# A list schedule made with other DMA constants and a pause between two engines' port operations

## The chip, the cores and the metric

The kernel runs on one core of a Trainium2 chip. The metric is the device time of one execution in microseconds (us), and a kernel's time is the median of its runs. Matrix products run on TensorE (PE in the rows), elementwise work and reductions on VectorE (DVE), ScalarE (ACT) and GpSimd (POOL); SyncE (SP) issues the DMA transfers in the order of its queue.

## The reference

One transformer-like block over 2048 tokens of 512 features: a layer norm, linear attention with a learned feature map (32 heads of 16), and a gate from a two-layer network of width 1792.

```python
def _A_ref(x, wqkv, w_phi, wo):
    qkv = (lambda x, *d: x.transpose(*d))((x @ wqkv).reshape(B, S, 3, H, Dh), 2, 0, 3, 1, 4)
    q, k, v = qkv[0], qkv[1], qkv[2]
    pq = jnp.einsum("bhsd,hdf->bhsf", q, w_phi)
    pk = jnp.einsum("bhsd,hdf->bhsf", k, w_phi)
    phi_q = jnp.concatenate([_softmax(pq, axis=-1), _softmax(-pq, axis=-1)], axis=-1)
    phi_k = jnp.concatenate([_softmax(pk, axis=-1), _softmax(-pk, axis=-1)], axis=-1)
    kv = jnp.einsum("bhsf,bhsd->bhfd", phi_k, v)
    z  = jnp.einsum("bhsf->bhf", phi_k)
    num = jnp.einsum("bhqf,bhfd->bhqd", phi_q, kv)
    den = jnp.einsum("bhqf,bhf->bhq", phi_q, z)[..., None] + 1e-6
    o = num / den
    return (lambda x, *d: x.transpose(*d))(o, 0, 2, 1, 3).reshape(B, S, D) @ wo
def _B_ref(x, w1, b1, w2):
    h = jnp.einsum("bsd,df->bsf", x, w1) + b1
    sp = jnp.log1p(jnp.exp(-jnp.abs(h))) + jnp.where(h > 0, h, jnp.zeros_like(h))
    return jnp.einsum("bsf,fd->bsd", h * jnp.tanh(sp), w2)
xn = _layernorm(x, axis=-1)
s = _A_ref(xn, A_wqkv, A_w_phi, A_wo)
g = _silu(_B_ref(xn, B_w1, B_b1, B_w2))
return x + s * g
```

## The kernel before

The kernel doesn't issue its instructions as it meets them. A class `Program` records every operation with its tiles, the engines that could do it, and what each would cost; `links` finds what depends on what; `simulate` plays the program through a model of the engines and gives every operation a start; `issue` then emits them in the order of these starts. All of them are emitted from one line, L372 (L371 in the changed kernel), so the rows are told apart by tiles.

The order has two levels. The string `ORDER` names the parts of the work, and TensorE does them in just that order. For the other engines, and for operations that either VectorE or GpSimd could do, the model decides, by when an operation is wanted. An operation that GpSimd is given gets a wait on the last VectorE operation that uses the port that the two share, when its planned start lies within `NEAR` ns of that one's end.

The parts that matter here: `N` normalizes a block of 128 tokens and transposes it on TensorE (tiles `x`, `st`, `mv`, `rs`, `nb`, `pt`); `Ka` to `Kd` are the k and v projections of a pair of blocks, built of seven products in place of eight from sums of weights (`ws1` to `ws4`, the v halves `wv0` and `wv1`) and differences of tokens (`xs`); `wk` and `wq` fold the feature map into the weights on TensorE (`wkf`, `wqf`). `A` accumulates k times v (`kvp`), `Q` projects q (`qx`, `qy`, `qz`), `D` and `U` are denominator and numerator (`pn`), `O` the output projection (weights `wor`, split in `wo`). `P` prepares a block of the first network weights (`w1a`, split in `w1ah`, `w1al`, `w1sh`, `w1sl`) and stores it, `M` loads it again (`w1b`), `Fa` to `Fd` are the four steps of the first network layer (`fx`, `fy`, `fz`; results `ha`, `hb`, `hc`, `hd`), `G` the second, `E` the end. Every product of two fp32 tiles is three matmuls of a high half and a low half: `fh` and `fl` are the halves of the transposed tokens, and `L` loads those of the second 1024 tokens from where they were stored (`xd`).

Tiles come out of pools with a fixed number of places. TensorE's accumulators are eight banks, used in turn: a product must wait until the engine that reads the bank's former content is done. Loads go into a pool of 38 places, and a load waits in SyncE's queue for the last reader of what its place held; what stands behind it in that queue waits too.

Of the kernel before, what the change touches and what calls it, by code (L numbers as in the profile page):

```python
# [27 lines left out]
NC = 8  # L28
PEN, HOLD, MARGIN, PTOL = -1000, 300, 1000, 0
BACK, COLD, DRATE, LANES, SWITCH = 1500, 3400, 300, 8, 300  # L30
BLOCK, HEAD, FETCH, IDLE = 256, 89, 5200, 2100
# [3 lines left out]
SLACK, AHEAD, LAT = 15000, 40000, 150  # L35
WAKE, NEAR = 13, 2500
ORDER = """
wk0 N6 N0 wv1 N1 wk1 wv0 N2 Ka0 Ka1 N3 ws Kb0 N7 b1 Kc0 N4 Kd0 wq0 wq1 N5 Kb1 P0 Kc1 Fa0 Kd1 A0 Ka2 Kb2 Kc2 Fb0 N8 N9
N10 Kd2 A1 Ka3 Kb3 Fc0 Kc3 N11 Kd3 N12 P5 A2 Ka4 Fd0 Kb4 Fa5 Fb5 Kc4 A3 N14 P4 Ka5 Fc5 Kd4 Kb5 Kc5 Fd5 N13 Fa4 Kd5 Fb4
A4 Fc4 N15 Ka6 Kb6 A5 Ka7 Kc6 Kb7 P3 P2 P6 Kc7 Kd7 Fa6 Kd6 Fa3 Fa2 Fb3 wQ Fb6 M0 Fc3 Fc6 Fd4 A6 P1 A7 Fa1 Fb2 Fd3 Q0  # L40
Fd6 Fc2 z D0 Fb1 Fc1 D1 L Q3 Q1 D2 Q2 Fa7 D3 Fb7 Fd1 Fd2 D4 M1 Q4 M3 Fc7 Fa10 Fd7 Fa8 D5 Fb8 D6 Fc8 M2 Fd8 D7 Fb10 Q7
M6 Fa9 D8 M5 Fc10 M4 Fb9 Q5 Fd10 Fc9 Q6 D9 Fa13 Fd9 Fa12 D10 Ub0 Fb13 Fb12 D11 Fc13 Fc12 D12 wo0 Fa11 wo1 Fb11 D13 Ua0
D14 Fc11 Fd13 O1 O4 O6 O7 R1 O0 O3 O5 R2 R0 Fd11 Fd12 G7 D15 Ua1 R4 G8 O2 Ub1 G14 G15 R5 O9 O15 O10 O8 G9 G16 R3 G17
G10 G11 R6 G12 G18 G19 G13 E1 G0 O14 G1 G20 E2 G2 O13 G3 G4 O11 G28 G5 G29 G30 G6 G31 G32 G33 G34 G35 E0 G21 G36 G22
G23 G24 E4 G37 G38 G39 G40 G41 G25 G42 G26 O12 E5 G27 G43 G44 G45 G49 E3 G46 G50 G47 G48 G51 E6 E7
"""
# [7 lines left out]
class Program:  # L54
# [105 lines left out]
    def links(self):  # L160
        ops = self.ops
        wr, rd = {}, {}
        for o in ops:
            o.succ, dep = [], set()
            for n in o.reads:
# [7 lines left out]
            if "PE" in o.impl:  # L173
                dep = {d for d in dep if "PE" not in ops[d].impl}
# [17 lines left out]
    def simulate(self, at):  # L192
# [20 lines left out]
        aset = 0  # L213
        half = False
        dma = port = told = 0
        code, fetched, cold = HEAD, 0, 0
# [24 lines left out]
        def go(o, e):  # L241
            nonlocal aset, dma, port, half, code, fetched, cold
            dur, calls = o.impl[e]
# [21 lines left out]
            if e in o.lock:  # L265
                dur += max(0, port - now)
                port = now + dur
            o.start, o.eng = now, e
# [5 lines left out]
            if e == "Q":  # L274
                if not lanes:
                    dur = 0
                    busy[e] = now
                nb = calls[0][1][0].free_size() * calls[0][1][0].shape[0] * 4
                dma = max(dma, now + (1100 if now > 2500 else 1350)) + nb / DRATE
                end = max(dma + 1000, now + 2000 + nb / 200)  # L280
                lanes.append(end)
                heapq.heappush(events, (dma - BACK, 2, -1))
# [16 lines left out]
        while left:  # L299
# [34 lines left out]
            for e in ("A", "V", "G", "Q"):  # L334
# [3 lines left out]
                while ready[e]:  # L338
                    late, i = heapq.heappop(ready[e])
                    o = ops[i]  # L340
                    if o.start is not None:
                        continue
                    if e in o.lock and port > now + PTOL:
                        held = True
                        skip.append((late, i))
                        if len(skip) > 60:
                            break
                        continue
# [31 lines left out]
def locks(e, m, a):  # L380
# [732 lines left out]
```

## Time and profile before

| what | value |
|---|---|
| time, median of 3 runs | 501.36 us (500.89 to 501.74) |
| time of the profiled execution | 501.55 us |
| its span, from the first to the last instruction | 499.8 us |
| TensorE busy | 487.7 us |
| VectorE, ScalarE, GpSimd busy | 443.6, 282.4, 271.1 us |
| moved by DMA | 105.69 MB, mean 211 GB/s |
| mean granted clock of TensorE | 0.991 |

The span is some 1.7 us shorter than the execution's time. Busy times of matmuls include a modelled end, so that those of successive matmuls overlap; how far apart they start is what one costs. The granted clock is a share of full speed (2.4 GHz); 0.50 is the lower level, 1.2 GHz.

### The profile page before, as it was taken

What the parts mean: (1) busy time and instruction counts of PE and PEld (TensorE: products, weight loads), DVE (VectorE), ACT (ScalarE), POOL (GpSimd) and SP (SyncE); (2) the same over time, 40 slices, a digit from 0 to 9 for tenths busy, and PEclk for the clock granted to TensorE, in tenths of its full rate; (3) what the DMA queues carried; (4) which work ended last, traced back from release to release, by engine and by line L of the source; (5) the groups of instructions that cost most, each with busy time, mean ns of one, the idle gap of its engine ahead of it and who ended that gap; (6) DMA issues with size and microseconds to landing.
All of it is one profiled execution on the core that took longest, in us unless ns stands there. A gap on an engine that the chain in (4) does not pass through costs nothing.

```text
span 499.8 us, 10023 instructions
## 1 busy us (share of the span) xinstructions
PE 487.7 (98%) x3690; PEld 424.3 (85%) x3690; DVE 443.6 (89%) x830; ACT 282.4 (57%) x433; POOL 271.1 (54%) x204
## 2 busy tenths in 40 slices
PE   8699999999999999999999999999999999999996
PEld 8478888878888889888898878778998899999996
DVE  6989999989999999999999989989587899768875
ACT  4676666445365552535243664487356888758611
POOL 4669997689688154889559497643020312112200
PEclk9799999999999999999999999999999999999999
DMA  8524438646979879888766286462644846644742
GB/s 303 185 92 161 148 97 297 220 190 171 358 287 321 298 257 337 306 274 285 251 216 231 100 289 225 170 211 94 201 133 148 269 150 191 207 150 139 255 154 85
DMA packets 68641, 105.69 MB, mean 211 GB/s; under 512 B 6896, under 2 KB 37744, under 8 KB 68592
## 3 DMA queue, kind: packets, MB, share of 16 engines
q1 hardware_dynamic: 68448, 104.79, 62.1%
q8 instruction: 29, 0.48, 0.4%
q10 hardware_dynamic: 144, 0.26, 0.2%
q14 instruction: 20, 0.16, 0.1%
HBM read 60.60 MB, written 44.43 MB: 210 GB/s over the span
## 4 chain that ended last, share of the span: by engine, by line
PE 91%; DVE 6%; ACT 2%; issue 1%; DMA 0%; DVEq 0%; ACTq 0%
PE y L372 28%; PE fx L372 15%; PE pw L372 9%; PE kx L372 8%; PE fy L372 7%; PE qx L372 5%; PE ky L372 4%; PE fz L372 4%; PE qy L372 2%; PE pn L372 2%; PE kz L372 2%; PE kvp L372 1%; PE pt L372 1%; PE qz L372 1%; PE wake L372 1%; PE wqf L372 1%
## 5 line engine op out<-in xcount | busy, mean ns | idle before, releaser
L372 POOL TENSOR_TENSOR r<-r 128x128 f32<-128x128 f32 (+1 forms) x18 | 10.2, 576 | 95.3 <-DVE r L372 56.6
L372 ACT ACTIVATE ah<-r 128x896 fp32r<-128x896 f32 (+1 forms) x56 | 46.8, 854 | 18.0 <-DVE r L372 9.4
L372 DVE TENSOR_TENSOR al<-r,ah 128x896 fp32r<-128x896 f32 (+1 forms) x45 | 46.3, 1047 | 9.1 <-ACT ah L372 4.9
L372 DVE TENSOR_TENSOR r<-r 128x128 f32<-128x128 f32 (+1 forms) x102 | 36.2, 384 | 6.8 <-ACT r L372 5.1
L372 ACT ACTIVATE r<-r 128x512 f32<-128x512 f32 x56 | 34.1, 624 | 14.1 <-DMA r<-hd 12.4
L372 PE MATMUL y<-w2t,ah 128*128 128x256 f32 x224 | 41.0, 283 | 0.0
L372 PE MATMUL fx<-fh,w1b 128*128 128x512 f32 x112 | 38.5, 392 | 0.0
L372 PEld LDWEIGHTS y<-w2t,ah 128*128 128x128 f32 x224 | 34.9, 192 | 0.2
L372 PE MATMUL y<-w2t,al 128*128 128x256 f32 x112 | 31.7, 283 | 0.0
L372 POOL TENSOR_TENSOR al<-r,ah 128x896 fp32r<-128x896 f32 (+1 forms) x11 | 20.1, 1829 | 21.0 <-ACT ah L372 9.5
L372 PE MATMUL y<-w2h,ah 128*128 128x256 f32 x96 | 27.2, 283 | 0.0
L372 PE MATMUL y<-w2l,ah 128*128 128x256 f32 x96 | 27.2, 283 | 0.0
L372 PE MATMUL y<-w2h,al 128*128 128x256 f32 x96 | 27.1, 283 | 0.0
L372 PEld LDWEIGHTS fx<-fh,w1b 128*128 128x128 f32 x112 | 21.0, 188 | 5.0 <-DVE ha L372 0.4
L372 PE MATMUL fx<-fl,w1b 128*128 128x512 f32 x56 | 21.9, 390 | 0.0
L372 PEld LDWEIGHTS y<-w2t,al 128*128 128x128 f32 x112 | 21.5, 192 | 0.2
L372 ACT ACT_TABLE_LOAD x13 | 16.7, 1283 | 6.9 <-DVE yy L372 5.5
L372 PE MATMUL y<-w2g,al 128*128 128x256 f32 x72 | 20.4, 283 | 0.0
L372 PE MATMUL y<-w2m,ah 128*128 128x256 f32 x72 | 20.4, 283 | 0.0
L372 PE MATMUL y<-w2g,ah 128*128 128x256 f32 x72 | 20.4, 283 | 0.0
L372 PE MATMUL fy<-fh,w1b 128*128 128x512 f32 x56 | 19.5, 389 | 0.0
L372 ACT ACTIVATE hb<-fx,b1t 128x512 f32<-128x512 f32 x14 | 9.6, 689 | 17.0 <-PE fx L372 14.5
(735 smaller groups left out, 1837.8 us busy)
## 6 DMA issues: line engine op xcount, KB each, us to landing
r<-hd SPq DMA_DIRECT2D x56, 256.0 KB, 3.5
xd<-xc SPq DMA_DIRECT2D x8, 896.0 KB, 5.5
w1b<-w1d SPq DMA_DIRECT2D x14, 512.0 KB, 4.6
w1b<-w1d SPq DMA_DIRECT2D x14, 384.0 KB, 4.3
so<-so SPq DMA_DIRECT2D x16, 256.0 KB, 2.6
x<-x SPq DMA_DIRECT2D x15, 256.0 KB, 4.0
w1a<-w SPq DMA_DIRECT2D x7, 512.0 KB, 5.4
w1d<-w1sh SPq DMA_DIRECT2D x7, 512.0 KB, 2.8
```

The lines of the kernel that those rows point to most:

```text
L372: ins = getattr(e, m)(*a, **k)
```

## The change

The string `ORDER` is another one, and the model that orders the other engines has other numbers. A transfer is planned to take its bytes at 400 instead of 300 bytes per ns and to land 1150 ns after that, where it was the later of 1000 ns after it and 2000 ns plus the bytes at 200 per ns after the issue; rows with short runs count as more bytes. `PTOL` is gone: after a VectorE operation that uses the shared port, GpSimd is now planned to start one only 140 ns (`GUARD`) after its end, and VectorE's are no longer stretched in the plan. `NEAR` goes from 2500 to 4000. `links` makes every operation on a tile of the pools depend on the tile's first operation. The instructions themselves stay as they were: TensorE has 2669 rows in both orders, SyncE 312 transfers in both, VectorE 815 and then 814.

```diff
-PEN, HOLD, MARGIN, PTOL = -1000, 300, 1000, 0
-BACK, COLD, DRATE, LANES, SWITCH = 1500, 3400, 300, 8, 300
+PEN, HOLD, MARGIN, GUARD = -1000, 300, 1000, 140
+BACK, COLD, DRATE, LANES, SWITCH = 1500, 3400, 400, 8, 300
-WAKE, NEAR = 13, 2500
+WAKE, NEAR = 13, 4000
 ORDER = """
-wk0 N6 N0 wv1 N1 wk1 wv0 N2 Ka0 Ka1 N3 ws Kb0 N7 b1 Kc0 N4 Kd0 wq0 wq1 N5 Kb1 P0 Kc1 Fa0 Kd1 A0 Ka2 Kb2 Kc2 Fb0 N8 N9
...
+wk0 N0 b1 N2 N1 N6 wv1 wk1 wv0 Ka1 ws Ka0 wq1 N3 Kb0 N7 N10 Kc0 P0 Kd0 N4 Kb1 N5 Kc1 Kd1 Fa0 Fb0 Fc0 A0 Ka2 Kb2 Kc2
...
     def links(self):
-        wr, rd = {}, {}
+        wr, rd, head = {}, {}, {}
         for o in ops:
-            o.succ, dep = [], set()
+            o.succ, dep = [], {head.setdefault(n, o.idx) for n in o.tiles if self.tag.get(n, "ps") != "ps"}
...
             if e in o.lock:
-                dur += max(0, port - now)
-                port = now + dur
+                port["V"], port["G"] = now + dur, now + dur + (GUARD if e == "V" else 0)
...
-                nb = calls[0][1][0].free_size() * calls[0][1][0].shape[0] * 4
-                dma = max(dma, now + (1100 if now > 2500 else 1350)) + nb / DRATE
-                end = max(dma + 1000, now + 2000 + nb / 200)
+                dma = max(dma, now + (1100 if now > 2500 else 1350)) + volume(calls[0][1]) / DRATE
+                end = dma + 1150
...
-                    if e in o.lock and port > now + PTOL:
+                    if e in o.lock and port[e] > now:
...
+def volume(aps):
+    runs = []
+    for v in aps[:2]:
+        n = 1
+        for st, c in reversed(list(v.ap)):
+            if st != n:
+                break
+            n *= c
+        runs.append(n)
+    return aps[0].free_size() * aps[0].shape[0] * (4 if min(runs) > 128 else 4.7)
```

The first place is TensorE's start, behind the first two foldings of the k weights. Before, three blocks of tokens are transposed (`pt`), then the other two foldings (`wkf`), then a fourth block:

```order
4 L372 MATMUL pt_151<-ident,x_146 128x128 x4
5 L372 MATMUL pt_157<-ident,x_152 128x128 x4
6 L372 MATMUL pt_166<-ident,x_161 128x128 x4
7 L372 MATMUL wkf_172<-phit,wkT_141 128x128 x4
8 L372 MATMUL wkf_173<-phit,wkT_142 128x128 x4
9 L372 MATMUL pt_182<-ident,x_177 128x128 x4
10 L372 MATMUL kx_183<-wv0h,fl_106 128x512
11 L372 MATMUL kx_183<-wv0l,fh_105 128x512
```

In the changed order all four blocks come ahead of the foldings:

```order
4 L371 MATMUL pt_151<-ident,x_146 128x128 x4
5 L371 MATMUL pt_157<-ident,x_152 128x128 x4
6 L371 MATMUL pt_163<-ident,x_158 128x128 x4
7 L371 MATMUL pt_171<-ident,x_166 128x128 x4
8 L371 MATMUL wkf_178<-phit,wkT_141 128x128 x4
9 L371 MATMUL wkf_179<-phit,wkT_142 128x128 x4
10 L371 MATMUL kx_183<-wv0h,fl_106 128x512
11 L371 MATMUL kx_183<-wv0l,fh_105 128x512
```

The foldings `wkf` stand closer to the first `kx`, and with them the copies that empty their banks.

The second place is VectorE at the first of these copies, the low half `wkl` of a folded k weight. Before, it stands as number 44, behind row statistics:

```order
40 L372 BN_STATS st_209<-x_208 128x6
41 L372 BN_AGGR mv_210<-st_209 128x2
42 L372 TENSOR_SCALAR rs_211<-mv_210 128x1
43 L372 BN_STATS st_221<-x_220 128x6
44 L372 TENSOR_TENSOR wkl_170<-wkf_172,wkh_169 128x512
45 L372 TENSOR_SCALAR nb_191<-mv_189,rs_190 128x1
46 L372 BN_AGGR mv_222<-st_221 128x2
47 L372 TENSOR_SCALAR rs_223<-mv_222 128x1
48 L372 BN_STATS st_240<-x_239 128x6
49 L372 TENSOR_TENSOR wkl_170<-wkf_173,wkh_169 128x512
```

In the changed order it is number 41:

```order
33 L371 BN_AGGR mv_204<-st_203 128x2
34 L371 TENSOR_SCALAR rs_205<-mv_204 128x1
35 L371 BN_STATS st_213<-x_212 128x6
36 L371 BN_STATS st_221<-x_220 128x6
37 L371 BN_AGGR mv_214<-st_213 128x2
38 L371 BN_AGGR mv_222<-st_221 128x2
39 L371 TENSOR_SCALAR rs_215<-mv_214 128x1
40 L371 TENSOR_SCALAR rs_223<-mv_222 128x1
41 L371 TENSOR_TENSOR wkl_176<-wkf_178,wkh_175 128x512
```

It has moved ahead by three places; of the two splits of v weights, the one of `wv0` has come to VectorE and the one of `wv1` has gone to GpSimd.

The third place is SyncE's queue where the token halves of the second 1024 tokens are loaded (`fh`, `fl` from `xd`). Before:

```order
100 L372 DMA hd_480<-hd_550 128x512
101 L372 DMA hd_551<-hc_535 128x512
102 L372 DMA fh_572<-xd 128x1024
103 L372 DMA kvw<-kvd 32x4x256
104 L372 DMA fl_573<-xd 128x1024
```

In the changed order the first low half `fl_612` stands there, and its place in the pool held `w1al_440`:

```order
101 L371 DMA hd_503<-hd_568 128x512
102 L371 DMA kvw<-kvd 32x4x256
103 L371 DMA fh_611<-xd 128x1024
104 L371 DMA hd_580<-ha_579 128x512
105 L371 DMA fl_612<-xd 128x1024
106 L371 DMA fh_613<-xd 128x1024
107 L371 DMA fl_614<-xd 128x1024
108 L371 DMA w1b_639<-w1d_443 128x768
```

On TensorE the last product with `w1al_440` is followed by two more of its kind and a q projection:

```order
739 L371 MATMUL fx_507<-fh_117,w1al_440 128x512
740 L371 MATMUL fx_507<-fl_118,w1ah_439 128x512
741 L371 MATMUL fx_507<-fh_117,w1ah_439 128x512
742 L371 MATMUL qx_598<-wqh_525,fl_106 128x256
743 L371 MATMUL qx_598<-wql_526,fh_105 128x256
```

Then comes the first reader of `fl_612`:

```order
781 L371 MATMUL qx_598<-wq1h,fl_118 128x256
782 L371 MATMUL qx_598<-wq1l,fh_117 128x256
783 L371 MATMUL qx_598<-wq1h,fh_117 128x256
784 L371 MATMUL fx_628<-fh_611,w1b_517 128x512
785 L371 MATMUL fx_628<-fl_612,w1b_516 128x512
786 L371 MATMUL fx_628<-fh_611,w1b_516 128x512
```

In the string, three q projections stand between `L` and `Fa7` before, and none in the changed one; there three matmuls of 128x512 and the last q projection lie between the release of the place and the reader.

## Rows read from the trace of the kernel before

**Rows 1.** The page, busy us, share of the span and instructions of two engines.

```profile
PE 487.7 (98%) x3690; PEld 424.3 (85%) x3690; DVE 443.6 (89%) x830; ACT 282.4 (57%) x433; POOL 271.1 (54%) x204
```

**Rows 2.** What TensorE waited for: us in all, times, longest.

```profile
PE kx L372 <- DVE wkl L372: 3.1, 1, 3.1
PE pt L372 <- ACT x L372: 2.2, 3, 1.1
PE wake L372 <- DVE mhalf L478: 1.1, 1, 1.1
PE kx L372 <- POOL wv0l L372: 1.0, 1, 1.0
```

**Rows 3.** Two windows: length, busy us by engine, granted clock, DMA share, GB/s.

```profile
20.00:26.00 6.00, 4.82 (x11) 3.84 (x12) 5.88 (x12) 1.98 (x4) 4.09 (x4) 0.50 0.02 4
...
120.00:480.00 360.00, 360.00 (x2732) 316.20 (x2731) 322.56 (x578) 206.89 (x310) 176.46 (x121) 1.00 0.68 227
```

**Rows 4.** TensorE's timeline: start, us, what; in brackets the idle time before it.

```profile
17.68 0.40 PE L372 MATMUL kz<-wv1h,fh 128*128 128x512 f32 x1
21.18 0.77 PE L372 MATMUL kx<-wv0h,fl 128*128 128x512 f32 x1 [3.10 <-DVE wkl L372]
...
30.99 0.66 PE L372 MATMUL pt<-ident,x 128*128 128x128 f32 x4 [1.06 <-ACT x L372]
31.41 0.48 PE L372 MATMUL kx<-ws3h,fl 128*128 128x512 f32 x1
...
41.49 0.39 PE L372 MATMUL ky<-ws1h,fl 128*128 128x512 f32 x1
```

**Rows 5.** VectorE's timeline, 16 to 24 us.

```profile
16.49 1.22 DVE L372 TENSOR_TENSOR ws<-ws,wvr 128x1024 f32<-128x1024 f32 x1
17.63 0.42 DVE L372 TENSOR_TENSOR fl<-xs,fh 128x256 fp32r<-128x256 f32 x1
17.96 0.42 DVE L372 TENSOR_TENSOR fl<-pt,fh 128x256 fp32r<-128x256 f32 x1
...
19.76 0.68 DVE L372 BATCH_NORM_STATS2 st<-x 128x6 f32<-128x512 f32 x1
20.36 0.67 DVE L372 TENSOR_TENSOR wkl<-wkf,wkh 128x512 fp32r<-128x512 f32 x1
...
23.56 1.61 DVE L372 TENSOR_TENSOR ws<-wvr,ws 128x1024 f32<-128x1024 f32 x1
```

**Rows 6.** The chain that ended last, in order of time: start, us, what.

```profile
36.26 3.57 PE wqf L372 x32
...
271.88 2.69 PE pn L372 x115
```

**Rows 7.** TensorE's timeline around the first q projection.

```profile
172.39 0.28 PE L372 MATMUL qx<-wqh,fl 128*128 128x256 f32 x1
...
177.55 0.40 PE L372 MATMUL fx<-fh,w1al 128*128 128x512 f32 x1
177.79 0.40 PE L372 MATMUL fx<-fl,w1ah 128*128 128x512 f32 x1
```

**Rows 8.** DMA issues of the whole trace: times, KB each, median us to landing.

```profile
w1b<-w1d SPq DMA_DIRECT2D x14, 512.0 KB, 4.6
...
fl<-xd SPq DMA_DIRECT2D x7, 512.0 KB, 6.6
...
wor<-wo SPq DMA_DIRECT2D x2, 512.0 KB, 4.8
```

**Rows 9.** The same view of the load issued at 199.67 us alone.

```profile
fl<-xd SPq DMA_DIRECT2D x1, 512.0 KB, 3.8
```

**Rows 10.** The same view of the load issued at 192.09 us alone.

```profile
fl<-xd SPq DMA_DIRECT2D x1, 512.0 KB, 8.1
```

**Rows 11.** The same view of the second load of the output weights, 286.83 us.

```profile
wor<-wo SPq DMA_DIRECT2D x1, 512.0 KB, 5.7
```

More of the change, by code (lines that the diff above doesn't have):

```diff
@@ L35 @@
 SLACK, AHEAD, LAT = 15000, 40000, 150
-WAKE, NEAR = 13, 2500
+WAKE, NEAR = 13, 4000
 ORDER = """
-wk0 N6 N0 wv1 N1 wk1 wv0 N2 Ka0 Ka1 N3 ws Kb0 N7 b1 Kc0 N4 Kd0 wq0 wq1 N5 Kb1 P0 Kc1 Fa0 Kd1 A0 Ka2 Kb2 Kc2 Fb0 N8 N9
[L39 to L45, printed above, removed]
+wk0 N0 b1 N2 N1 N6 wv1 wk1 wv0 Ka1 ws Ka0 wq1 N3 Kb0 N7 N10 Kc0 P0 Kd0 N4 Kb1 N5 Kc1 Kd1 Fa0 Fb0 Fc0 A0 Ka2 Kb2 Kc2
+Fd0 P5 Kd2 A1 Ka3 N11 N8 Fa5 Kb3 N9 P4 N12 Kc3 Fb5 Fc5 A2 Fd5 Kd3 Ka4 Fa4 Kb4 Kc4 Kd4 N13 Fb4 A3 Ka5 Kb5 Kc5 Kd5 Fc4
+Fd4 P6 Fa6 A4 N14 N15 P1 Ka6 Kb6 wq0 P3 A5 Ka7 Kc6 Kd6 Kb7 P2 Kc7 Kd7 Fb6 Fa3 Fb3 Fa1 A6 Fb1 Fc6 Fc1 M0 Fc3 A7 wQ Fd6
+Q0 Q1 z Fd3 D0 D1 Fa2 Q2 Fd1 D2 Q3 L D3 Fa7 D4 Fb2 Fc2 M1 Fa8 Fd2 Fb7 M3 D5 Fb8 Fc8 D6 M6 Fc7 Q4 Fd7 D8 Fa10 Fd8 Fb10
+M2 Q7 Q5 Q6 Fa13 Fa9 Fb13 Fb9 D7 Fc10 Fc13 D9 D10 wo1 D11 M4 Fc9 Ua0 Fd13 Fd9 Fa11 Fb11 wo0 M5 R0 Fd10 Fa12 D12 Fb12
+Fc11 Fc12 Ub0 Fd12 R1 Fd11 D13 G7 O3 O5 O0 O7 R2 O2 O1 D14 R3 O6 D15 Ub1 O4 G8 Ua1 R6 R5 G0 G1 G9 O13 R4 O14 G10 G2
+G11 G3 G4 G12 G5 G6 G13 G14 E0 O9 O12 G15 G16 G17 G18 G19 G28 G20 G29 E1 E2 O15 O10 O8 G30 G42 G31 G32 G33 G43 G34 O11
+G35 G44 E4 G36 G21 G45 G46 G22 G47 G48 G37 G23 G38 E6 G39 G40 G24 G25 G26 G41 G27 E5 E3 G49 G50 G51 E7
 """
@@ L214, in simulate @@
         half = False
-        dma = port = told = 0
+        dma = told = 0
+        port = {"V": 0, "G": 0}
         code, fetched, cold = HEAD, 0, 0
@@ L241, in go @@
         def go(o, e):
-            nonlocal aset, dma, port, half, code, fetched, cold
+            nonlocal aset, dma, half, code, fetched, cold
             dur, calls = o.impl[e]
@@ L359, in simulate @@
                     heapq.heappush(ready[e], s)
-                if held and port > told:
-                    told = port
-                    heapq.heappush(events, (port, 2, -1))
+                if held and port[e] > told:
+                    told = port[e]
+                    heapq.heappush(events, (told, 2, -1))
         return sorted(ops, key=lambda o: (o.start, o.idx))
```

## The prediction

> **What bounds the kernel now.** I read the page's busy shares first: TensorE is busy for 487.7 of 499.8 us, VectorE for 443.6 [rows 1]. So a change of order can only give back what TensorE does not work, and the next view, what TensorE waited for, says how little that is: four entries, 7.4 us in all, the longest 3.1 us for VectorE's copy `wkl` and three waits of together 2.2 us for normalized rows `x` [rows 2]. The windows say where: from 20 to 26 us the granted clock is 0.50, the lower of its two levels, and from 120 to 480 us TensorE is busy for all of 360.00 us [rows 3]. Its timeline of the start shows the mechanism. The last product of `kz` starts at 17.68; the next `kx`, at 21.18, needs an accumulation bank in which a folded weight `wkf` still lies, and VectorE empties it only with `wkl`. What is at stake is thus the start (some 7 us of waits and the slow stretch behind the longest of them), against the risk of opening a wait in a stretch that has none.
>
> **The change, part by part.** No instruction is added or taken away that counts. The constants act through the order alone, so I follow the order at two places.
>
> *The start, VectorE.* In before, VectorE reaches `wkl` at 20.36 and ends it at 21.03, and TensorE starts 0.15 us later [rows 4, 5]. In the changed order `wkl` comes after fewer things. Steps cost 1.14 us (128x1024), 0.60 (128x512 and a row statistic) and 0.33 (128x256), which are the distances between starts [rows 5]; the smallest ones I put at 0.1. From the first sum `ws`, which I place at 9.9, nineteen instructions stand ahead of `wkl`: two, five and six of the three sizes and six small ones, 2.3 + 3.0 + 2.0 + 0.6 = 7.9 us, 17.8. With 0.7 us for waits on rows that land I take 18.5, and 19.25 for TensorE's second `kx`: 1.9 us earlier than 21.18. By itself this is a lead of 1.9 us.
>
> *The start, what is late next.* The changed order has two things more before TensorE's product with `ws3h`: two of the four folds of the q weights (four take 3.57 us in before [rows 6], so 1.79) and one more transposition (0.42 from 30.99 to 31.41 [rows 4]). I carry the chain on with the same prices: TensorE comes to `ws3h` at about 31.1. Before, it is there at 31.41, having done 2.2 us less: a lead of 2.5 us. But then its transposition of row block 4 takes the bank that VectorE empties with the fortieth instruction after `wkl`, a subtraction into `xs`. Ahead of that stand three of 1.14, thirteen of 0.60, fourteen of 0.33, one of 0.44 (a scaling of 512 columns, my estimate from its neighbours) and nine small ones: 3.4 + 7.8 + 4.6 + 0.4 + 1.0 = 17.2. From 18.5 that is 35.7, and 36.0 at its own end; with 0.4 for short waits on ScalarE and GpSimd I take 36.4. TensorE would have been ready at 35.3, so 1.1 us are lost there. Four more instructions (2.2 us) lead to the addition into `v1`, which releases the bank for `ky` with `ws1h`, at 38.65. Before, that product starts at 41.49, after all four folds [rows 4]; with 1.79 us for the two not yet done, the lead is 41.49 − 38.65 − 1.79 = **1.05 us**. Its bounds: 2.5 if VectorE is not late (the copies then being a little faster than I counted), 0 if it loses another microsecond. I take 1.0, since all steps are rows of the same form. The folds that were put off stand later on TensorE and cost there what they save here.
>
> *The middle, the reload of the tokens.* In before the first low half of the second token half, `fl_573`, is asked for some 21 us of matmuls (counted along the order) ahead of its first reader. In the changed order `fl_612` stands in SyncE's queue behind the last product with `w1al_440`, whose place it takes, and its first reader comes soon: two more products of 128x512, one q projection of 42 products, one product. A product is 0.24 us (177.55 to 177.79) and a q projection with its change of form 5.16 us (172.39 to 177.55) [rows 7], so 0.48 + 5.16 + 0.24 = 5.9 us. The load takes 6.6 us in the median of seven [rows 8]; 3.8 at the front of a burst [rows 9] and 8.1 inside one [rows 10]. With 0.1 us to issue, TensorE waits 0.8 us by the median, nothing by the fast end, 2.3 by the slow one. `fl_612` stands near the front of its burst (only `fh_611` goes well ahead of it), so I take **0.5**.
>
> *The middle, the output weights.* The second load of `wo` now stands one group of `pn` (2.69 us [rows 6]) and eighteen products (4.32) ahead of the product that waits for what ScalarE does behind it: a 128x1024 split and one eviction, some 1.7 us (my estimate from VectorE's 1.14 and 0.60 for such sizes). 7.0 − 0.1 − 1.7 leaves 5.2 for a load that takes 4.8 in the median of its two [rows 8] and 5.7 as the slower of them [rows 11]. Bounds are 0 and 0.5; I take **0.2**.
>
> *The planned pause.* VectorE operations that ran into GpSimd's are visible: a `ws` of 128x1024 took 1.61 us against a distance of 1.14 for its like [rows 5]. TensorE waits for VectorE nowhere after the start [rows 2], so time that VectorE gains there is worth nothing at the end, and 0.14 us of pause cost nothing either, as GpSimd has the slack. Covered by the same fact: instructions moved between the two engines. If that cover is gone, a collision of half a microsecond shows in full.
>
> *Sum.* The profiled execution took 501.55 us: 499.8 of span and 1.75 around it. −1.0 (start) + 0.5 (tokens) + 0.2 (`wo`) gives 501.25, and as that execution lies 0.19 above the median of 501.36, **501.1** for a median.
>
> **The rule of the Trainium skill that bears on this.** The page "DMA: Bandwidth & Descriptors", section "Anatomy of one DMA — SWDGE (gpsimd) path", gives 2.0 us and bytes/436e3 for one transfer, an estimate of 3.2 us for the 512 KB of `fl`. It is stated for another queue than the one here. By it both waits of the middle would be nothing and the sum 500.4. The trace disagrees: no load of that size has a median under 4.6 us, and `fl` has 6.6 [rows 8].
>
> **The rivals.** *Faster:* the reloads land as at the front of the burst (3.8 us [rows 9]); the start keeps its 1.0 and the time is 500.4; if VectorE is also in time at row block 4, the lead is 2.5 and the time 498.9. For it speaks that the changed burst begins with the queue nearly empty; against it that further loads follow within a few microseconds. Chance 0.31.
>
> *Slower, by one mechanism:* the schedule now believes that a lone load of 512 KB lands 3.6 us after it is issued (1100 + 524288/400 + 1150 ns), while before it believed 4.6 (2000 + 524288/200), and the rows say 4.6 to 6.6 [rows 8]. So loads stand late in the queue, and TensorE waits for the first reader of `fl_612`. At 8.1 us [rows 10] that wait is 2.3, and with 0.5 at `wo` the time is 501.36 − 1.0 + 2.3 + 0.5 = 503.2. It decides from a landing of some 7.6 us on: there the wait is 1.8, and with 0.2 at `wo` it outweighs the lead of 1.0 by the 1.0 that can be told. Against it: most such loads land sooner. A place that I did not follow, where VectorE's work is now needed earlier, would look the same in the total. Chance 0.27.
>
> *No change:* the lead of the start is returned in the middle, in whole or for the greater part, or never arises; 500.4 to 502.4. This is my forecast's own case, chance 0.42.
>
> **How the numbers follow.** A measurement of this kernel can tell about 0.2%, 1.0 us, from no change. The forecast 501.1 lies within that of 501.36, its own range 500.4 to 502.3. Faster than 500.36 is the first rival, slower than 502.36 the second: 0.31, 0.42, 0.27. The range leaves out a tenth at each end: 499.2 (a little short of the whole lead of the start) and 503.2 (both loads at their slow ends).
>
> **What the profile after would show.** Right: `wkl` on VectorE near 18.5 and the second `kx` near 19.3; a wait of about 1 us of a transposition for VectorE near 35 us; `ky` with `ws1h` near 38.7; waits of TensorE for `fl<-xd` near 198 us and for ScalarE near 275 us, together about 0.7 us. Wrong: TensorE waiting in the first 10 us for the second part of the k weights, whose load now goes out one row block later; no wait at row block 4; a wait for the reload above 2 us; or a wait for VectorE in the stretch from 120 to 480 us, where the order before has none.

## The result, and the profile of the changed kernel

The changed kernel takes **503.11 us** in the median of 7 runs (502.11 to 503.67), the kernel before 500.89 beside it (499.62 to 501.74, 7 runs): a ratio of 1.0047, interval 1.003 to 1.0065, so slower by some 2 us. A second measurement (e1 below) gives 1.0046 (1.0027 to 1.0065). The forecast was no change, 501.1, which is 0.3 below the 501.36 that it started from; the kernel went up by 2.2, as its slower rival says. That 503.11 still lies inside the range (499.2 to 503.2), at its upper end, is owed to the base: 501.36 is 0.5 to 1.8 us above the medians of the kernel before in all later measurements.

Executions of the kernel before come in two kinds by clock: of the fourteen beside e1, nine have a mean granted clock of 0.994 to 0.999 and take 499.5 to 501.0 us, and five, like the one that the prediction was read from (501.55, 0.991), have 0.991 or 0.992 and take 501.2 to 502.0.

The profiled execution of the changed kernel took 502.11 us (span 500.3), the least of its seven. The page's busy line, against [rows 1]: TensorE does the same work, VectorE 4.6 us less, and nothing came of it.

```profile
PE 487.8 (98%) x3690; PEld 423.5 (85%) x3690; DVE 439.0 (88%) x833; ACT 278.2 (56%) x430; POOL 269.7 (54%) x204
```

What TensorE waited for, against [rows 2]. The wait for `wkl` is only 0.5 us shorter; two waits for `xs` are new, and one for ScalarE's eviction `hd`.

```profile
PE kx L371 <- DVE wkl L371: 2.6, 1, 2.6
PE wqf L371 <- DVE xs L371: 1.6, 1, 1.6
PE wake L371 <- DVE mhalf L490: 1.1, 1, 1.1
PE pt L371 <- ACT x L371: 0.8, 2, 0.6
PE pt L371 <- DVE xs L371: 0.8, 1, 0.8
PE fz L371 <- ACT hd L371: 0.5, 1, 0.5
```

The windows, against [rows 3]: 20 to 26 us at a mean of 0.72, and half a microsecond lost where there had been none.

```profile
20.00:26.00 6.00, 4.89 (x19) 3.73 (x17) 5.91 (x15) 2.75 (x5) 3.46 (x3) 0.72 0.00 0
120.00:480.00 360.00, 359.51 (x2795) 315.20 (x2795) 317.51 (x577) 205.58 (x313) 172.26 (x120) 1.00 0.65 222
```

TensorE's timeline at the places of [rows 4], taken from the trace of e5 (the changed kernel but for three instructions near 278 us, which do not bear on the start), where the clock of this stretch was full:

```profile
16.34 0.39 PE L383 MATMUL kz<-wv1h,fh 128*128 128x512 f32 x1
19.37 0.47 PE L383 MATMUL kx<-wv0h,fl 128*128 128x512 f32 x1 [2.64 <-DVE wkl L383]
...
26.50 1.13 PE L383 MATMUL wqf<-phit,wqT 128*128 128x128 f32 x8 [2.28 <-DVE xs L383]
...
31.44 0.48 PE L383 MATMUL kx<-ws3h,fl 128*128 128x512 f32 x1
...
36.67 0.63 PE L383 MATMUL pt<-ident,x 128*128 128x128 f32 x4 [0.90 <-DVE xs L383]
...
38.83 0.50 PE L383 MATMUL ky<-ws1h,fl 128*128 128x512 f32 x1 [0.15 <-DVE v L383]
```

In the changed kernel's own trace, with the clock at 0.72, VectorE comes to `wkl` as forecast:

```profile
18.55 0.68 DVE L371 TENSOR_TENSOR wkl<-wkf,wkh 128x512 fp32r<-128x512 f32 x1
```

The second `kx` starts at 19.37 too, `ws3h` at 31.46, the transposition at 36.66 and `ky` at 38.81. The start is therefore as it was worked out (19.25, 31.1, 36.4, 38.65), and it does not depend on TensorE's clock: what TensorE gains at full clock it gives back as a longer wait for `xs` (2.28 instead of 1.6). VectorE sets it.

DMA issues of the whole trace, against [rows 8]: `w1b` has gone from 4.6 to 6.2.

```profile
w1b<-w1d SPq DMA_DIRECT2D x14, 512.0 KB, 6.2
w1b<-w1d SPq DMA_DIRECT2D x14, 384.0 KB, 6.3
fl<-xd SPq DMA_DIRECT2D x7, 512.0 KB, 6.1
wor<-wo SPq DMA_DIRECT2D x2, 512.0 KB, 5.4
```

Two windows show what goes with it; the last three columns are granted clock, DMA share and GB/s. First the changed kernel:

```profile
200.00:240.00 40.00, 40.00 (x211) 34.51 (x210) 38.51 (x74) 15.31 (x24) 35.32 (x24) 1.00 1.01 383
260.00:290.00 30.00, 29.53 (x246) 23.45 (x245) 28.80 (x54) 14.05 (x24) 19.63 (x12) 1.00 0.83 270
```

Then the kernel before:

```profile
200.00:240.00 40.00, 40.00 (x225) 35.11 (x224) 37.82 (x70) 19.57 (x30) 34.56 (x25) 1.00 0.86 293
260.00:290.00 30.00, 30.00 (x267) 24.94 (x266) 28.25 (x56) 14.50 (x26) 21.97 (x15) 1.00 0.55 194
```

The changed order packs the traffic of the middle into 200 to 240 us and fills the DMA engines there entirely (in the windows of 20 us beside it the share is 0.47 ahead and 0.12 behind, against 0.91 and 0.65 before). The loads of `w1b` of 512 KB that lie in this window land after 6.7 us in the median, and after 5.3 in the kernel before.

The reload that the forecast priced is not late: `fl_612` lands 3.9 us after its issue, 1.8 us ahead of its first reader, which follows its predecessor at the usual distance of 0.23.

```profile
194.76 0.32 SPq L371 DMA_DIRECT2D fl<-xd  x1
...
200.25 0.40 PE L371 MATMUL fx<-fh,w1b 128*128 128x512 f32 x1
200.48 0.40 PE L371 MATMUL fx<-fl,w1b 128*128 128x512 f32 x1
```

The place near 278 us, in the changed kernel's timeline of all engines: the load of `wo` is issued at 271.69, ScalarE can split it at 277.43 and then makes the two evictions `hd`, and TensorE, which is through with the product of 278.25 about 0.23 us later, starts `fz` only at 279.12.

```profile
271.69 0.38 SPq L371 DMA_DIRECT2D wor<-wo  x1
...
277.43 1.06 ACT L371 ACTIVATE wo1h<-wor 128x1024 fp32r<-128x1024 f32 x1 [12.04 <-DMA wor<-wo]
...
278.25 0.39 PE L371 MATMUL fx<-fh,w1b 128*128 128x512 f32 x1
278.39 1.25 ACT L371 ACTIVATE hd<-fx,b1t 128x512 f32<-128x512 f32 x2
...
279.12 0.50 PE L371 MATMUL fz<-fh,w1b 128*128 128x512 f32 x1 [0.47 <-ACT hd L371]
```

### The profile page after: what moved, and what is told of

Read it like the earlier page. It is cut to its first block, busy times and chain, and to the rows that moved or that the text cites. A ratio compares the mean times of both kernels' runs of the same rounds, so it can differ in the third digit from the quotient of the medians.

```text
span 500.3 us, 9989 instructions
## 1 busy us (share of the span) xinstructions
PE 487.8 (98%) x3690; PEld 423.5 (85%) x3690; DVE 439.0 (88%) x833; ACT 278.2 (56%) x430; POOL 269.7 (54%) x204
## 4 chain that ended last, share of the span: by engine, by line
PE 89%; DVE 5%; DMA 2%; POOL 2%; issue 1%; SPq 0%; ACT 0%; ACTq 0%; POOLq 0%; DVEq 0%
PE y L371 28%; PE fx L371 15%; PE pw L371 9%; PE fy L371 8%; PE kx L371 7%; PE qx L371 5%; PE ky L371 4%; PE fz L371 4%; PE qy L371 2%; PE kvp L371 2%; PE kz L371 2%; PE pn L371 2%; PE qz L371 1%; DMA wor<-wo 1%; DMA x<-x 1%; PE pt L371 1%
## 5 line engine op out<-in xcount | busy, mean ns | idle before, releaser
L371 DVE TENSOR_TENSOR al<-r,ah 128x896 fp32r<-128x896 f32 (+1 forms) x50 | 47.8, 976 | 8.7 <-ACT ah L371 6.8
L371 DVE TENSOR_TENSOR r<-r 128x128 f32<-128x128 f32 (+1 forms) x106 | 34.7, 357 | 8.9 <-ACT r L371 4.5
L371 POOL TENSOR_TENSOR r<-r 128x256 f32<-128x256 f32 (+1 forms) x14 | 8.7, 621 | 57.3 <-DVE r L371 44.8
L371 POOL TENSOR_TENSOR al<-r,ah 128x896 fp32r<-128x896 f32 (+1 forms) x6 | 11.1, 1857 | 47.1 <-ACT ah L371 26.7
L371 DVE TENSOR_REDUCE tz<-ez 128x64 f32<-128x1024 f32 x16 | 19.2, 1198 | 0.0
```

The costliest lines, as they stand in the source:

```text
L371: ins = getattr(e, m)(*a, **k)
```

## The experiments

Medians in us; "before" is the kernel before on the same chip, measured beside the run (e5 to e8, f5 and f6 ran on another chip than the rest). Each kernel is the changed one, or the one before, with the edit shown. Where an edit moves instructions, `r` is the finished order, and `find` picks instructions from it by engine and tile, `move` puts one ahead of another, and `delay` puts some of them, with what depends on them, behind a later one. These helpers are left out of the cuts.

| | median (runs) | before | ratio, interval |
|---|---|---|---|
| e1 changed kernel again | 503.25 (7) | 500.35 | 1.0046, 1.0027 to 1.0065 |
| e2 kernel before again | 501.33 (1) | 500.35 | |
| e3 new string, old model | 522.46 (6) | 500.35 | 1.0446, 1.0421 to 1.047 |
| e4 old string, new model | 515.49 (6) | 500.35 | 1.0293, 1.026 to 1.0325 |
| e5 `wo` split behind | 503.55 (10) | 500.17 | 1.0059, 1.004 to 1.0078 |
| e6 `wkT01` ahead | 503.36 (8) | 500.17 | 1.0042, 1.0025 to 1.0059 |
| e7 `wkl` ahead | 504.66 (6) | 500.17 | 1.0072, 1.0051 to 1.0094 |
| e8 before, `wkT01` behind | 499.90 (12) | 500.17 | 0.999, 0.9973 to 1.0007 |
| e9 readers of the reload behind | 502.42 (12) | 499.58 | 1.0049, 1.0034 to 1.0063 |
| e10 `wo` load early | 502.12 (12) | 499.58 | 1.0047, 1.0032 to 1.0062 |
| e11 small products together | 503.34 (7) | 499.58 | 1.0063, 1.0039 to 1.0086 |
| e12 VectorE relieved | 503.79 (7) | 499.58 | 1.0062, 1.004 to 1.0085 |
| f1 work added at 213 us | 504.15 (6) | 499.76 | 1.0078, 1.0056 to 1.01 |
| f2 work added at 277 us | 503.31 (6) | 499.76 | 1.0075, 1.0047 to 1.0104 |
| f3 work added at 399 us | 505.12 (6) | 499.76 | 1.01, 1.0074 to 1.0126 |
| f4 before, work added at 213 us | 502.38 (12) | 499.76 | 1.0049, 1.0028 to 1.0069 |
| f5 work added at both places | 504.93 (6) | 500.00 | 1.0106, 1.0076 to 1.0135 |
| f6 before, a wait filled | 501.52 (12) | 500.00 | 1.0026, 1.0007 to 1.0044 |

### e1 and e2: both kernels once more

No edit.

> The changed kernel once more, to see whether the waits of its first profile come again. Theory A (loads that the model believes to land too early are waited for): TensorE waits for ScalarE behind the load of wo near 278 us again, 0.5 to 1.5 us, and in a run that is slower than 502.1 also for fl<-xd near 198 us, up to 2 us. Theory B (the order of VectorE's and GpSimd's work is what costs): no wait at loads, and other waits of TensorE for VectorE or GpSimd, of together 1 to 2 us. Time 502 to 504 by both.

> The kernel before once more, for a second profile of it. Both theories: waits of TensorE only in the first 31 us, about 9 us of lost time there, and nothing over 0.3 us later; time 500 to 501.5.

The loss is there again, and the waits of both traces are in the main those of the first ones: with the changed order TensorE waits near 278 us for ScalarE (0.6 us, theory A) and at the start for VectorE, and near 198 us for nothing. The trace of e2 (501.33 us, clock 0.992) is again one with the lower clock, 20 to 26 us at 0.51.

### e3 and e4: one half of the change each

e3 is the kernel before with the new string; e4 the changed kernel with the old one.

```diff
 ORDER = """
-wk0 N6 N0 wv1 N1 wk1 wv0 N2 Ka0 Ka1 N3 ws Kb0 N7 b1 Kc0 N4 Kd0 wq0 wq1 N5 Kb1 P0 Kc1 Fa0 Kd1 A0 Ka2 Kb2 Kc2 Fb0 N8 N9
+wk0 N0 b1 N2 N1 N6 wv1 wk1 wv0 Ka1 ws Ka0 wq1 N3 Kb0 N7 N10 Kc0 P0 Kd0 N4 Kb1 N5 Kc1 Kd1 Fa0 Fb0 Fc0 A0 Ka2 Kb2 Kc2
...
```

> The new ORDER string with the model of before (its DMA constants, no pause, NEAR 2500, no head dependence). TensorE's order is that of the changed kernel, word for word; the load of wo has over 11 us in place of 5.5 us of matmuls. Theory A: the wait near 278 us is gone and the time comes down to 500.0 to 501.5. Theory B (the string costs): as slow as the changed kernel, 502.5 to 503.5.

> The old ORDER string with the new model. TensorE's order is that of before. Theory A: some load is waited for, and the time is 1 to 2 us over before, 502 to 503. Theory B (the string costs): as before, 500.5 to 501.5.

Both theories fall: neither the string nor the model carries the change alone, either half without the other costs 15 to 22 us. TensorE then waits all over for whoever feeds it. e3, its first waits:

```profile
PE fy L372 <- DVE hc L372: 3.0, 2, 1.7
PE fx L372 <- DVE k14e L372: 2.6, 1, 2.6
```

e4, the same:

```profile
PE y L371 <- DVE yy L371: 2.4, 1, 2.4
PE kx L371 <- ACT fh L371: 2.1, 1, 2.1
```

String and model are fitted to each other. The question of the 2 us is thus not which constant is right, but where this one pair loses them.

### e5: the split of wo behind two evictions

```diff
+        wo = find("A", "wo1h")
+        move(find("A", "hd13"), wo)
+        move(find("A", "hd9"), wo)
```

> The changed kernel with one difference: ScalarE evicts the two hidden blocks hd13 and hd9 ahead of the split of the second half of wo, which waits for its load; no instruction is added. Load theory (TensorE waits at 278 us for ScalarE, which waits for that load): the wait fz <- ACT hd, 0.5 to 0.6 us in two traces, is gone and the median falls by 0.5 to 502.6. If in the untraced runs the load is later still than in the traced ones: a fall of 1 to 2 us. Start theory (the loss is in the first 40 us): the wait is gone from the trace and the median stays within 0.3 us of 503.2.

The wait at 278 us is gone, and two others take its place at 284 and 286 us (0.37 for VectorE's `ha`, 0.45 for `ol`). No gain. Behind the first of them stands a collision of two engines. GpSimd splits off the low half of `wo`, by the edit half a microsecond later than in the changed kernel (278.62 there), and a VectorE operation that falls into this takes 2.23 us, where the median of its sixteen is 0.18. From its end VectorE works without a gap up to the `ha` that TensorE waits for.

```profile
279.11 2.39 POOL L383 TENSOR_TENSOR wo1l<-wor,wo1h 128x1024 fp32r<-128x1024 f32 x1 [5.12 <-ACT wo1h L383]
279.32 2.23 DVE L383 SCALAR_TENSOR_TENSOR den<-tz 128x32 f32<-128x32 f32 x1
...
283.69 0.67 DVE L383 TENSOR_TENSOR ha<-ha,fz 128x512 f32<-128x512 f32 x1
```

In the changed kernel's own trace the same operation takes 1.72 us at 279.35, and the wait at 278 covers it. A late split of `wo` can thus hold TensorE up in two ways, and e5 closes only one.

### e6 and e8: the load of the second k weights

e6 moves it ahead in the changed kernel, e8 behind in the kernel before.

```diff
+        move(find("Q", "wkT01"), find("Q", "x6"))
```

> The changed kernel with one difference: the load of the second part of the k weights (wkT01) is issued ahead of the load of row block 6, as in the kernel before it was issued ahead of its third row block. Start theory (in most runs this load lands late, TensorE's second fold wkf waits for it and the whole start moves): the second wkf starts 0.5 to 1 us earlier, the median falls by 1 to 2 us to 501.5 to 502.2. VectorE theory (the chain of copies and subtractions sets the start, loads don't): the fold starts earlier, but the second kx stays at 19.4 us and the median within 0.3 us of 503.2, or above it if row block 6 is now late.

> The kernel before with one difference: the load wkT01 is issued behind the third row block's load instead of ahead of it, which is where the changed kernel has it. Start theory: TensorE waits for it in the first 12 us, and the time rises by 1 to 2 us over 500.4, with that about half or more of the loss of the changed kernel is explained. VectorE theory: TensorE has a wait of some 0.5 us there, which the later wait for wkl swallows; no change within 0.3 us.

No effect in either, so the start theory falls: the second `kx` stays (19.56 in e6). This was also one of the signs that the prediction named as "wrong", and TensorE does wait for this load, 0.5 to 1.4 us in most traces of the changed order, but VectorE's `wkl` covers it. e8 gives something else: a trace of the old order from an execution with the higher clock (500.12 us, 0.994). There 20 to 26 us have 0.72 instead of 0.50, and `ky` with `ws1h` starts 1.26 us earlier than in [rows 4].

```profile
20.00:26.00 6.00, 5.07 (x17) 4.02 (x18) 5.88 (x13) 1.75 (x4) 3.85 (x4) 0.72 0.01 4
```

```profile
40.23 0.39 PE L386 MATMUL ky<-ws1h,fl 128*128 128x512 f32 x1
```

### e7 and e12: VectorE at the start

e7 moves `wkl` ahead of the statistics of four row blocks (and ScalarE's `wkh` ahead of `ws1h`); e12 gives three of VectorE's instructions to ScalarE.

```diff
+        move(find("A", "wkh1", "wkf3"), find("A", "ws1h"))
+        last = find("V", "wkl1", "wkf3")
+        for o in [o for o in r[:r.index(last)] if o.eng == "V" and any(t.split("_")[0] in ("st3", "mv3", "st7", "mv7", "st10", "mv10", "st4") for t in o.tiles)]:
+            r.remove(o)
+            r.insert(r.index(last) + 1, o)
+            last = o
```

```diff
+        for n in (("wqf1", "wqf2"), ("x10", "nb10"), ("v1", "kx0")):
+            find("V", *n)[0].eng = "A"
```

> The changed kernel with one difference: on VectorE the two copies wkl that empty the folds' banks stand ahead of the row statistics of four later row blocks, and ScalarE's copy wkh ahead of the one of ws1h. If the wait for wkl is what the start costs: the wait of 2.6 us at kx falls to under 1, the granted clock stays at full level behind it, and the time falls by 2 us to about 501. If VectorE is busy throughout up to row block 4, so that the order within its queue only moves the wait: kx starts about 2 us earlier, the later waits for xs grow by as much, and the median stays within 0.5 us of 503.2.

> The changed kernel with three instructions of the first 30 us moved from VectorE to ScalarE (the copy of a folded q weight, the normalization of row block 10, the copy of v1), 1.7 us of VectorE's time behind wkl and ahead of the subtraction that row block 4's transposition waits for. VectorE theory (VectorE, busy from 10 to 40 us without a gap, sets TensorE's start): the wait of 0.8 us for xs near 35.4 us is gone, the product ky with ws1h starts at 37.9 instead of 38.8, and the median falls by 0.9 to 1.0 to 502.3. If the start is not what is lost, or ScalarE is late in its place: no change within 0.3 us.

e7 takes the wait for `wkl` down to 0.3 us and is 1.4 us slower than e1; the second `kx` starts at 16.82, and the waits come back in the next groups of products, for the same engine:

```profile
PE wqf L386 <- DVE v L386: 3.1, 1, 3.1
PE wqf L386 <- DVE xs L386: 2.2, 1, 2.2
...
PE kx L386 <- DVE wkl L386: 0.3, 1, 0.3
```

Up to there the second reading is right: the fold that waits for `xs` starts at 26.34, in the changed kernel's trace at 26.49. But behind it this trace (506.31 us, the slowest of e7's six) loses 2.5 us more by something else than VectorE, which is busy for 3.72 of the next 6 us only: the granted clock is 0.50 there, against 1.00 in the changed kernel's trace.

```profile
26.00:32.00 6.00, 5.66 (x19) 5.04 (x20) 3.72 (x9) 3.57 (x6) 3.75 (x6) 0.50 0.18 73
```

`ky` with `ws1h` starts at 41.30 instead of 38.81. All six executions of e7 have a mean clock of 0.991 to 0.993, so the lower clock may be what they all lose by; where it falls in the other five is not recorded.

In e12 the `wqf` copy, put behind `ws4h` on ScalarE, holds up the normalized rows behind it, and VectorE, ahead now, waits 1.24 us at 31.29 for a product; `ky` starts at 39.23. So the second reading of e12 is right in its reason, though the median lies 0.5 above e1, not within 0.3: VectorE's queue is full from 10 to 40 us, but taking work off it at those places only lets ScalarE be late. What a better order of the start would be is left open.

e12 gave more: its profiled execution took 504.35 us, and shows waits for loads in the middle that the first traces of the changed order do not have: the first product below stands 0.50 us behind its predecessor of 215.38 (0.23 is usual), the second 0.63.

```profile
215.88 0.47 PE L387 MATMUL fx<-fh,w1b 128*128 128x512 f32 x1
...
220.72 0.50 PE L387 MATMUL fy<-fl,w1b 128*128 128x512 f32 x1 [0.24 <-DMA fl<-xd]
```

The two loads of `w1b` issued at 206.28 landed in 8.3 us in the median (6.7 in the changed kernel's own trace), and the load of `wo` in 6.3 (5.6). In the twelve traces of the changed order other than e7's that pair takes 6.6 to 8.8 us; the three with 8.2 or more (e10, e12, f3) lose 0.2 to 0.7 us at 215 and 0.4 at 220 us, the nine with 7.8 or less nothing (two of them, f1 and f5, have work added just ahead). Window for window: TensorE is idle 0.35 us from 200 to 240 and 1.44 us from 260 to 290, against nothing and 0.47.

```profile
200.00:240.00 40.00, 39.65 (x203) 33.42 (x203) 37.91 (x73) 14.96 (x23) 34.26 (x23) 1.00 1.00 383
260.00:290.00 30.00, 28.56 (x242) 22.64 (x241) 28.80 (x51) 13.99 (x24) 19.09 (x13) 1.00 0.75 249
```

### e9, e10 and e11: one place of the middle each

e9 puts the first two groups that read the reloaded tokens behind the four that followed them; e10 issues the load of `wo` ahead of one of `w1b`; e11 puts the key-value products of two pairs of row blocks side by side, as before.

```diff
+        fa7 = find("PE", "fx7", "w1b00") + find("PE", "fz7", "w1b00")
+        delay(fa7, find("PE", "fy2", "w1sh2")[-1])
```

```diff
+        o = find("Q", "wor1")[0]
+        r.remove(o)
+        r.insert(r.index(find("Q", "w1b34")[0]), o)
```

```diff
+        delay(find("PE", "kvp", "k12e"), r[r.index(find("PE", "kvp", "k14e")[0]) - 1])
```

> The changed kernel with one difference: the two groups of six products that first read the reloaded tokens (fx_628 and fz_629 with w1b) stand behind the four groups with w1sl/w1sh that followed them, 24 products or 5.4 us later; the loads themselves stay. Reload theory (in the executions whose trace was not kept these loads land later, and TensorE waits for them): the median falls by 0.5 to 1.1 us, to 502.1 to 502.7, and the runs scatter less. If the loads land in time in nearly all executions, as in four of the five traces: no change within 0.3 us of 503.3.

> The changed kernel with one difference: the load of the second half of wo stands ahead of a load of w1b and a store in SyncE's queue, whose place in the buffers it takes, and so goes out some 5 us earlier. Load theory: the wait of TensorE near 278 us (0.6 to 0.9 us with the slower product behind it) is gone and none takes its place at 283 us, the median falls by 0.6 to 0.9 to 502.4 to 502.7. If the load of w1b, which now goes out in its place, is late itself: the wait moves to a product with w1b near 282 us, no change.

> The changed kernel with one difference: the key-value products of the seventh pair of row blocks (k12e, k13e) stand right ahead of those of the eighth (k14e, k15e), as in the kernel before, instead of 12 us earlier. Form theory (TensorE loses about 0.3 us each time it goes from 512-column products to the small ones and back: 0.09 before, 0.11 and 0.11 behind them in the trace of the kernel before, and the changed order does so once more): the median falls by 0.3 to 502.9. If only waits for other engines count: no change.

Measured against the kernel before of the same chip (0.6 us lower than beside e5 to e8), none is a clear gain over e1: e9 lies 2.8 us above it, e10 2.5, e11 3.8, e1 2.9. e9 thus agrees with the traces, in which the reload's first readers don't wait. In e10 the load goes out only 1 us earlier (270.66), since its buffer is not free sooner; the wait at 278 is gone, but in the same execution TensorE waits at 216.26 for `w1b` (0.56). In e11 the 0.3 us that go with a change between large and small products did not come back as time; in its trace TensorE, freed of the small products, waits 0.29 us at 157.70 for ScalarE's `ha`, so what the change of form costs by itself stays open.

### f1 to f5: added work as a gauge

Moving one place at a time does not say what the executions lose whose trace is not kept. Work of known length does: where TensorE waits, added products cost nothing until the wait is filled.

```diff
+        o, p = find("PE", "fy7", "fh31")[0], find("PE", "fx7", "fh41")[0]
+        ps, (u, v) = o.impl["PE"][1][0][1][0], p.impl["PE"][1][0][1][1:3]
+        o.impl["PE"] = o.impl["PE"][0], [("matmul", (ps, u, v), dict(start=True, stop=True, skip_group_check=True))] * 8 + o.impl["PE"][1]
```

In f2 `o` and `p` are the first product of `fx11`, in f3 that of `pw10`; f5 has the edits of f1 and f2; f4 is f1's edit in the kernel before.

> The changed kernel plus work: eight more products of 512 columns (1.81 us at 0.227 each) ahead of the first product into fy7, near 213 us, between the issue of the reloads and of the w1b loads of this stretch and their readers at 215 and 220 us; their result is overwritten by the product that follows. Load theory (in most executions TensorE waits there 0.5 to 1.6 us, as in two of the traces): the added work fills the wait, and the median rises by 0.2 to 1.3 us only, to 503.5 to 504.6. If the loads land in time in most executions: the whole 1.8, to 505.1.

> The changed kernel plus the same eight products (1.81 us) ahead of the first product into fx11, near 277 us, between the issue of the load of wo and the product fz11 that waits for what ScalarE does behind it. Load theory: the wait of 0.6 to 1.4 us and the slower product behind it are filled, and the median rises by 0.3 to 1.1, to 503.6 to 504.4. If that wait is only in the traced executions: 505.1.

> The changed kernel plus the same eight products (1.81 us) ahead of the first product into pw10, near 399 us, where no trace has a wait: the control. Both theories: the whole 1.8, a median of 505.1 (504.8 to 505.4).

> The kernel before plus the same eight products (1.81 us) ahead of its first product into fy7, behind its reload of the tokens. Load theory: its loads land with room, so nothing is filled, and the median rises by the whole 1.8, 502.0 where the kernel before has 500.2. If the kernel before waits for loads there too: less than 1.3.

> The changed kernel with both groups of eight added products, near 213 and near 277 us: 3.63 us of added work. If the loads of the two places are what the changed order loses and their waits are separate, the two swallow 1.0 + 1.8 as each alone, and the median is 503.3 + 3.6 - 2.8 = 504.1. If the two runs with one group swallowed the same loss: 505.1. If a load holds up by chance and nothing is swallowed on this chip: 506.9.

The control f3 rises by 1.9 over e1 (505.12 against 503.25), as the added work is long. Against it, f2 is lower by 1.81, the whole of the added work, and f1 by 0.97. f5, with 1.81 more work than f3, is 0.19 lower: 2.0 us of 3.6 are swallowed, less than the 2.8 that two separate losses would give. These are medians of six runs that scatter (f2 502.54 to 506.24, f3 503.98 to 507.54). Drawn again and again from these runs, the 1.81 of f2 lies between −1.0 and 3.2, the 0.97 of f1 between −0.1 and 2.3, and the 2.0 of f5 between 0.1 and 3.4 (95%). So the gauge shows that f5 swallows something; how much, and how it is shared between the two places, it does not settle.

The traces fit it. That of the control (505.49 us) has the waits for loads of e12: it loses 0.2 us at 215.90, 0.4 at 220.73 and 0.85 at 280.69. It also has one near 142 us that the first traces hardly have: TensorE waits for ScalarE's `v`, and ScalarE had waited for a load of `w1a`. This wait is 0.2 to 0.5 us in four of the twelve traces (e10, e11, f1, f3).

```profile
140.72 0.85 ACT L388 ACTIVATE w1ah<-w1a 128x768 fp32r<-128x768 f32 x1 [2.75 <-DMA w1a<-w]
...
142.59 0.50 PE L388 MATMUL kx<-ws3h,xc 128*128 128x512 f32 x1 [0.40 <-ACT v L388]
...
280.69 0.50 PE L388 MATMUL fz<-fh,w1b 128*128 128x512 f32 x1 [0.69 <-ACT hd L388]
```

In the trace of f5 (505.04 us) no wait for a load is left from 200 to 290 us:

```profile
200.00:240.00 40.00, 40.00 (x204) 34.20 (x204) 37.42 (x71) 14.50 (x23) 33.46 (x22) 1.00 1.00 383
260.00:290.00 30.00, 30.00 (x249) 24.18 (x248) 26.77 (x51) 13.92 (x22) 18.93 (x12) 1.00 0.76 246
```

The kernel before (f4) swallows nothing: its median rises by 2.6, more than the work added; five of its twelve executions have a clock of 0.992 or 0.993 and 503.5 to 505.5 us, why is open.

Its kept trace (500.77 us) has the quickest start of all traces of the old order: the clock falls from 14.5 to 18 us, ahead of the wait for `wkl` (1.46 us there), and is full from 20 on.

```profile
10.00:16.00 6.00, 4.19 (x25) 3.39 (x25) 5.50 (x13) 5.53 (x11) 4.49 (x2) 0.90 1.05 406
16.00:20.00 4.00, 2.92 (x8) 1.96 (x7) 3.93 (x11) 3.49 (x6) 2.61 (x2) 0.72 0.80 210
20.00:24.00 4.00, 3.48 (x17) 2.63 (x17) 3.85 (x10) 1.42 (x2) 3.34 (x3) 1.00 0.00 0
```

```profile
38.97 0.39 PE L389 MATMUL ky<-ws1h,fl 128*128 128x512 f32 x1
```

### f6: what TensorE does ahead of the slow stretch

The kernel before with the first product into `kx` issued eight times, which fills the wait of 1.7 us for `wv0l`.

```diff
+        o, p = find("PE", "kx0", "wv0h")[0], find("PE", "kx0", "wv0h")[0]
+        ps, (u, v) = o.impl["PE"][1][0][1][0], p.impl["PE"][1][0][1][1:3]
+        o.impl["PE"] = o.impl["PE"][0], [("matmul", (ps, u, v), dict(start=True, stop=True, skip_group_check=True))] * 7 + o.impl["PE"][1]
```

> The kernel before with the first product into kx (wv0h, fl) issued eight times instead of once, its result overwritten each time: TensorE fills with it the wait of some 1.7 us for GpSimd's wv0l at 13 to 15 us. Nothing else moves, and TensorE then waits for VectorE's wkl as before, so by waits alone the time stays at 500. If what TensorE does at 13 to 19 us decides at which clock it works from 20 to 26 us: the granted clock of 0.50 in that stretch gives way to a higher one or becomes the rule, and the median moves by up to 1 us either way, to 499.0 or 501.3.

The wait for `wv0l` is gone, nothing else moved, and the median rises by 1.5: six of twelve executions now have a clock of 0.991 and 501.4 to 502.6 us, where the kernel before beside it has four of seventeen at 0.991 or 0.992. The other six take 500.0 to 501.7. What TensorE does from 13 to 15 us may thus decide how often the old order runs its slow stretch behind the wait for `wkl`. It is not shown: six of twelve against four of seventeen can be chance (one in seven), and the other six, too, are some 0.5 us slower than their like beside them.

## Why the prediction was wrong, by its steps

*The start, VectorE and what is late next: right.* `wkl` starts at 18.55 (18.5 forecast), the second `kx` at 19.37 (19.25), the transposition of row block 4 waits 0.8 us (1.1), `ky` with `ws1h` starts at 38.81 (38.65). In the twelve traces of the changed order other than e7's it lies between 38.2 and 39.2, whatever the clock.

*The lead of 1.0: wrong in its base. This is the first step that failed.* The lead was measured from an execution with 20 to 26 us at the lower of TensorE's two clock levels, 1.2 GHz [rows 3]. In the old order TensorE sets the pace behind `wkl`, so the clock counts there: `ky` at 41.49 and 41.58 with that stretch at 0.50, 40.23 at 0.72, 38.97 at 1.00. The changed order, with two folds (1.79 us) still to do, stands at 40.6. Its lead is 0.9 against the first, −0.4 against the second, −1.6 against the third (one trace), and the kernel before is mostly not of the first kind: 67 of its 96 executions beside the experiments have a mean clock of 0.994 or more. Its medians in the six measurements are 499.6 to 500.9, not the 501.36 of three runs that the sum was made against.

*The loads of the middle, 0.5 and 0.2: the second step that failed.* The 0.5 stood at `fl_612`, and there nothing is lost. Its distance to the reader was right (5.7 us, forecast 5.9 with 0.1 to issue), but the load lands after 3.6 to 4.2 us in all thirteen traces of the changed order, as at the front of a burst [rows 9]. What is late stands behind it in the same burst and was put at nothing: the `w1b` and the low half that are read at 215 and 220 us cost 0.6 to 1.1 us together in three of the ten traces without work added there, and nothing in seven. A load of `w1a` near 142 us, put at nothing too, costs up to 0.5. At `wo` the mechanism was right and the size wrong: TensorE loses 0.6 to 1.6 us in the eight traces with that place as it is, against 0.2 with bounds of 0 and 0.5; in the changed kernel's own trace the load takes 5.6 instead of 4.8 and what follows it 1.8 instead of 1.7. In all, the middle lost about 2.0 us in the median by the gauge of f5, rough as it is, not 0.7.

The landings were taken from rows of before [rows 8 to 11], where the DMA engines are busy for 0.86 of 200 to 240 us. The change itself fills them to 1.01, and later loads land later: 6.2 for `w1b` instead of 4.6, 6.6 to 8.8 for the two at 206 us. The sentence on the Trainium skill ("DMA: Bandwidth & Descriptors", "Anatomy of one DMA — SWDGE (gpsimd) path"), an estimate of 3.2 us for 512 KB, is further off still: no median of these loads is under 4.5 in any trace of the changed order.

*The planned pause: nothing in the changed kernel's trace.* From 120 to 480 us it has only the wait at 278. But the cover is thin, as the prediction said it might be: in e5, where that wait is gone, the collision behind it shows as 0.37 us.

*The sum.* From the trace of e8 (span 498.4) to that of the changed kernel (500.3) are 1.9 us: 0.4 at the start (38.81 + 1.79 − 40.23), 0.7 at `wo`, 0.3 between TensorE's last product and the end (4.8 to 4.9 us in all traces of the changed order, 4.5 in all of the old one), and some 0.5 in pieces of 0.1 to 0.3 that are not taken apart. What the medians have beyond that (they lie 2.2 and 2.9 apart) fits the loads of executions like those of e12 and f3, as f1 to f5 gauge them. That each untraced execution waits at just these loads is argued, not seen.

*The rivals.* "Slower, by one mechanism" is what happened in its result and in its kind: loads are asked for so late that TensorE waits for what they bring, at a price near its 2.3 + 0.5, with the start returning nothing. But the place that it named, `fl_612`, went as its opposite, the faster rival, says. That this follows from the constant for the landing is not shown: e4 changed too much else.

## What to carry to other kernels

A schedule that asks for its loads just in time must be priced with the landings that it causes, not with those of the schedule before: look at the DMA share of the stretch into which it packs them. Before pricing a lead at a place where the granted clock is low, find out whether all executions have that clock there, and which engine sets the pace in the changed order; a faster TensorE is worth nothing where VectorE does. In a burst of loads, price those at its end too, not the first alone. Where single traces cannot show what a median loses, work of known length, put in front of a suspected wait and at a control place, gauges it; with six runs each the answer here was good to some 1.7 us only.

## What the runs showed of the hardware that was not expected

A fall of the clock cost nothing where it came ahead of a wait that TensorE had anyway (f4: 0.72 from 16 to 20 us, and the quickest start of the old order), and some 2.5 us where it came behind one (e7: 0.50 from 26 to 32 us). Filling a wait of TensorE made the kernel before slower by 1.5 us (f6); why is open. The loads of one pair, at the same place of the changed order or of an edited form of it, took 6.6 to 8.8 us from one trace to the next, while the first low half of the same burst always took 3.6 to 4.2. A VectorE operation of 0.18 us took 2.23 beside one of GpSimd that took 2.39 (e5).
